# Block sums of the keys of two head pairs: two more columns of the turning matmul, or a reduction from PSUM

## The chip, the cores and the metric

The kernel runs on one core of a Trainium2 chip. A core has TensorE (PE, matmuls, with its weight loads shown apart as PEld), VectorE (DVE), ScalarE (ACT), GpSimd (POOL) and SyncE (SP), each with an instruction stream of its own; they meet through semaphores. TensorE writes into PSUM, which VectorE and ScalarE read; all engines but TensorE's output use the core's SBUF memory, and DMA queues move data between it and the chip's main memory. The metric is the device time of one execution in microseconds (us), lower is better.

## The reference

```python
def _attn_ref(q, k, v):                  # each (4, 8, 768, 64)
    B, H, S, D = q.shape
    block = 64; n_blocks = S // block; top_k = 3; scale = 1.0 / np.sqrt(D)
    k_rep = k.reshape(B, H, n_blocks, block, D).mean(axis=3)
    gate_scores = np.einsum('bhsd,bhnd->bhsn', q, k_rep)
    causal = pos[:, None] // block >= np.arange(n_blocks)[None, :]
    gate_scores = np.where(causal, gate_scores, -1000000000.0)
    top_idx = np.argsort(gate_scores, axis=-1)[..., -top_k:]
    # query i sees the keys j <= i in its three top blocks and in its own block
    scores = scale * np.matmul(q, k.transpose(0, 1, 3, 2))
    scores = np.where(mask, scores, -1000000000.0)
    attn = np.exp(scores - np.max(scores, axis=-1, keepdims=True))
    attn = attn / (np.sum(attn, axis=-1, keepdims=True) + 1e-09)
    return np.matmul(attn, v)

def _moe_ref(x, w_in, w_out):            # x (3072, 512), w_in (512, 2048), w_out (2048, 512)
    h = x @ w_in
    g = 0.5 * h * (1.0 + np.tanh(c * (h + 0.044715 * h * h * h)))
    return g @ w_out
```

The output of the attention, with the heads put side by side, is the input of the two matmuls with the gelu between them. The gate needs, for each head, the mean of the keys of each of the 12 blocks of 64; since only the order of the gate's scores matters, a sum serves as well as a mean. These sums over the keys are what the change is about.

## The kernel before, in words

The heads go in 16 pairs, p = 4 b + hp for batch b and pair of heads hp. Pairs 0 to 3 (batch 0) start the kernel; while TensorE later does the two matmuls of one batch, the attention of the next batch runs beside it.

*A pair of batch 0* (`pre`, from L528 on, and `heads2`). The loads bring keys, queries and values with the sequence on the partitions (`load`, L387; `load_0`, L421, for the first pair, its queries from ScalarE's queue and its keys from SyncE's). TensorE turns the keys in two halves of three chunks of 128 x 128 in f32 (`turn`, L538 or L541), into one PSUM bank per half. A copy takes the turned half to SBUF as f16 (`turned`; a copy is at L356 on ScalarE, L358 on GpSimd and L360 on VectorE). `ksb_h` puts the sums of a half's six blocks into a small matrix `ksb`, laid out by a 0/1 mask so that both heads of the pair can be gated at once; for pair 0 the sums of the second half also go into `ksbx`, because pair 0 gates in two steps. The queries are turned in the same way (L541), copied in f32, and cast once more to f16 for the scores (`q16`, on GpSimd for pairs 1 to 3). The gate is four f32 matmuls (L680, eight records), then VectorE does the selection: a 32 x 32 transpose (L696), the causal addition (L703), the three largest by MAX8 (L712), a comparison (L713) and the mask (L717). TensorE turns the mask (L749) and a copy brings it to SBUF. Then the scores (L856), the exponentials on ScalarE (L875) into one of six buffers `ats`, GpSimd's select for the causal part (L901), and the product with the values (L924), which are cast to f16 on GpSimd (`cast_v`). VectorE divides (L942, L943), TensorE turns the result (L981) into `xT`.

*The block sums before the change.* For the pairs named in KSUM (0 and 1), the matmul that turns a chunk of keys takes `identk` as its moving operand, which is the 128-wide identity with two more columns that hold ones for the chunk's first and second 64 keys. So it writes 130 columns, the last two of them block sums, and one VectorE multiplication (L588) by the mask reads them from PSUM. For pairs 2 and 3 the turning is a plain f32 transpose (L541), and VectorE reduces the 384 turned columns in PSUM to six sums (L576) and multiplies them by the mask (L582).

*The batches 1 to 3* load with a transposing pattern (L393), turn by VectorE (L557), reduce from SBUF (L614, L631), and use a score matmul with the mask as extra rows (L1039), exponentials (L1052), selects (L1066) and products (L1078).

*The two matmuls.* `s1` (L1115) multiplies by w_in, gelu on ScalarE (L1127); it waits for the last exponential of its batch, the turned result `xT` and its half of w_in. `s2_plain` (L1315) multiplies by w_out for batch 0; the last batch uses further forms (L1204, L1365, with joins on VectorE at L1414). The weights come in two halves each, 1 MB a half, issued by GpSimd (`load_w`, L453); the issue of w_in waits for the last values of batch 0 through a small copy (L451).

*What sets the order.* The program builds a numbered list of operations, and `Plan.run` emits them by a written-out list, ORDER: the instructions of each engine stand in the order of that list. BUFFER picks the buffer where several serve, and ENGINE names the operations that go to ScalarE or GpSimd and not to the engine they name first. SyncE's and GpSimd's DMA issues are operations in the same list. `warm` (L1517) are filler matmuls on zeros; the list holds them where TensorE was planned to have nothing else to do. NK = 3 sets of `ks` and `ksb` rotate over the pairs, and a third kind of PSUM bank ("pre", three of them) is held from a turning until the copy and the sums have read it.

Of the kernel before, what the change touches and what calls it, by code (L numbers as in the profile page):

```python
# [182 lines left out]
    "POOL": [  # L183
        337, 586, 587, 646, 647, 707, 708, 972, 973, 1035, 1036, 1097, 1159,
        1160, 1425, 1426, 1488, 1489, 1551, 1613]}


class Op:
# [1431 lines left out]
```

## Time and profile before

| | |
|---|---|
| time, median of 3 runs | 254.39 us (254.17 to 254.81) |
| the profiled execution | 253.93 us |
| its span, first to last instruction | 252.2 us |
| granted TensorE clock, mean | 1.000 |
| PE busy | 244.2 us (97%) |
| DVE busy | 188.8 us (75%) |
| ACT busy | 177.5 us (70%) |
| POOL busy | 84.0 us (33%) |

How to read the profile's lines. The first part of the page gives each engine's busy time, its share of the span and its instructions. A line of slices cuts the span in 40; a digit is the busy share in tenths, and PEclk is the clock granted to TensorE. A row of the windows gives a stretch (from:to, its length), then the busy time of PE, PEld, DVE, ACT and POOL with their counts, the granted clock, the DMA share and GB/s. A row of the groups names a line of the kernel, the engine, the operation, output and input, shapes and count, then busy us and mean ns of one, and the idle time before them with what ended it. A row of the timeline gives the start and the length in us of a run of like instructions on one engine, what they are, how many (x), and in brackets the idle time before them and what ended it. The chain is the work that ended last, followed back from the end; its summary gives shares by engine, with a q behind an engine's name for its queue or sequencer. Matmul records overlap, so that six in a row take less than six times one.

### The profile page before, as it was taken

How to read it: one execution, taken by the hardware profiler on the slowest of the kernel's cores; microseconds unless marked ns; L12 is line 12 of the kernel's file. 1: busy time of each engine (PE TensorE's matmuls, PEld its weight loads, DVE VectorE, ACT ScalarE, POOL GpSimd, SP SyncE). 2: the span in 40 equal slices, each digit the busy share in tenths (PEclk: the TensorE clock that was granted, in tenths of full speed). 3: DMA queues.
4: the chain of work that ended last, by engine and by line, in shares of the span. 5: the costliest groups of instructions: out<-in, count | busy, mean ns of one | idle time of the engine just before them, and what ended most of it. 6: DMA issues, size and time to landing. Idle time of an engine off the chain costs nothing.

```text
span 252.2 us, 6437 instructions
## 1 busy us (share of the span) xinstructions
PE 244.2 (97%) x2484; PEld 170.2 (67%) x2484; DVE 188.8 (75%) x535; ACT 177.5 (70%) x226; POOL 84.0 (33%) x166
## 2 busy tenths in 40 slices
PE   6899999999999999999999999999999999999993
PEld 4677776555555565565778887656777887666883
DVE  2679851034789999999997998999876585688954
ACT  2498978545899899867899795576999936656200
POOL 8657860011237657112147561210147500000000
PEclk9999999999999999999999999999999999999999
DMA  7998699999989987999899667184121330100023
GB/s 159 218 200 184 97 213 198 205 156 151 153 140 164 155 170 127 146 138 261 151 182 162 137 109 140 27 214 99 26 86 28 90 120 30 65 22 0 4 106 144
DMA packets 130927, 32.62 MB, mean 129 GB/s; under 512 B 124528, under 2 KB 126928, under 8 KB 130896
## 3 DMA queue, kind: packets, MB, share of 16 engines
q1 hardware_dynamic: 126160, 27.62, 62.8%
q0 software_dynamic: 3136, 4.19, 9.8%
q10 hardware_dynamic: 1600, 0.39, 0.8%
q8 instruction: 19, 0.31, 0.5%
q14 instruction: 12, 0.10, 0.1%
HBM read 27.26 MB, written 6.29 MB: 133 GB/s over the span
## 4 chain that ended last, share of the span: by engine, by line
PE 80%; SPq 8%; DMA 4%; DVE 3%; POOL 2%; issue 1%; DVEq 0%; POOLq 0%
PE wide L1115 27%; PE bank L1365 22%; PE wide L1039 9%; SPq L387 7%; PE bank L1315 6%; PE wide L1204 6%; PE bank L1078 5%; DMA vsd<-in_v_dram 2%; PE bank L680 2%; SPq L393 2%; DMA sd<-in_k_dram 1%; DMA G<-in_q_dram 1%; PE bank L924 1%; PE wide L856 1%; PE bank L981 1%
## 5 line engine op out<-in xcount | busy, mean ns | idle before, releaser
L1115 PE MATMUL wide<-xT,w_in 128*128 128x384 f16 x416 | 74.8, 326 | 0.0
L1052 ACT ACTIVATE ats<-wide 128x896 f16<-128x896 f32 x72 | 63.1, 915 | 5.8 <-PE wide L1039 3.8
L1127 ACT ACTIVATE G<-wide 128x768 f16<-128x768 f32 x52 | 42.0, 810 | 27.4 <-PE wide L1115 23.1
L1115 PEld LDWEIGHTS <-w_in 128*128 128x128 f16 x416 | 39.9, 98 | 26.9 <-issue 1.0
L1066 POOL TENSOR_SCALAR_AFFINE_SELECT ats<-ats 128x256 f16<-128x256 f16 x72 | 31.0, 443 | 51.1 <-ACT ats L1052 37.5
L1039 PE MATMUL wide<-qT,kT 76*128 76x512 f16 (+3 forms) x192 | 38.8, 305 | 0.0
L557 DVE STREAM_TRANSPOSE s<-sd 128x768 f32<-128x768 f32 x24 | 23.2, 971 | 14.2 <-DMA sd<-in_k_dram 12.9
L1365 PE MATMUL bank<-w_out,G 128*128 128x256 f16 x216 | 32.6, 272 | 0.0
L1365 PEld LDWEIGHTS <-G 128*128 128x128 f16 x288 | 26.9, 98 | 5.5
L1315 PE MATMUL bank<-w_out,G 128*128 128x512 f16 x96 | 28.8, 379 | 0.0
L358 POOL CAST kT<-s 64x768 f16<-64x768 f32 x20 | 16.9, 855 | 33.0 <-DVE s L557 32.4
L1414 DVE TENSOR_TENSOR osb<-bank,osb 128x512 f32<-128x512 f32 (+1 forms) x38 | 22.2, 592 | 4.7 <-PE bank L1365 4.1
L1078 PEld LDWEIGHTS <-ats 128*128 128x128 f16 x504 | 22.8, 98 | 4.2
L1078 PE MATMUL bank<-v,ats 128*128 128x65 f16 x504 | 24.9, 194 | 0.0
L1039 PEld LDWEIGHTS <-kT 76*128 76x128 f16 x192 | 17.2, 98 | 9.8 <-issue 0.3
L875 ACT ACTIVATE ats<-wide 128x1024 f16<-128x1024 f32 (+3 forms) x24 | 20.8, 916 | 3.2 <-PE wide L856 3.0
L1365 PEld LDWEIGHTS <-XS 128*128 128x128 f16 x216 | 20.1, 97 | 4.3
L1365 PE MATMUL bank<-TS,XS 128*128 128x256 f16 x144 | 22.6, 272 | 0.0
L358 POOL CAST v<-vsd 128x768 f16<-128x768 f32 x13 | 11.1, 858 | 22.9 <-DMA vsd<-in_v_dram 15.7
L962 DVE TENSOR_TENSOR xn<-bank,zr 128x384 f16<-128x384 f32 x24 | 13.4, 557 | 0.8
L712 DVE MAX8 sel<-sel 128x8 f32<-128x12 f32 x160 | 13.3, 157 | 0.6
L356 ACT CAST qT<-s 64x768 f16<-64x768 f32 x15 | 12.4, 830 | 0.3
(118 smaller groups left out, 352.8 us busy)
## 6 DMA issues: line engine op xcount, KB each, us to landing
out_dram<-osb SPq DMA_DIRECT2D x23, 256.0 KB
vsd<-in_v_dram SPq DMA_DIRECT2D x26, 192.0 KB
sd<-in_k_dram SPq DMA_DIRECT2D x48, 96.0 KB
sd<-in_q_dram SPq DMA_DIRECT2D x48, 96.0 KB
w_in<-in_moe_w_in_dram POOLq DMA_DIRECT2D x2, 1024.0 KB, 11.6
w_out<-in_moe_w_out_dram POOLq DMA_DIRECT2D x2, 1024.0 KB, 20.6
G<-in_k_dram SPq DMA_DIRECT2D x6, 192.0 KB
TS<-in_v_dram SPq DMA_DIRECT2D x6, 192.0 KB
```

The costliest lines, as they stand in the source:

```text
L358: nc.gpsimd.tensor_copy(out=out, in_=in_)
L557: nc.vector.transpose(out=T[key + "T32", p], in_=T[key, p].rearrange("p t j -> p (t j)"))
L875: nc.scalar.activation(out=T["at", u][:, :, 0:n], in_=plan.buf[("st",) + u].rearrange("p (h w) -> p h w", h=2)[:, :, 0:n], func=AF.Exp, bi ...
L1039: nc.tensor.matmul(st[:, x:e], kT16[i][h][0:76, s0:s0 + 128], qT16[i][h][0:76, s0 + (x - cb):s0 + (e - cb)], start=True, stop=True)
L1052: nc.scalar.activation(out=T["at", u][:, 0:n], in_=plan.buf[("st",) + u][:, 0:n], func=AF.Exp, bias=0.0, scale=SCALE)
L1066: nc.gpsimd.affine_select(out=dg, in_=dg, compare_op=ALU.is_ge, fill=0.0, base=0, pattern=[[0, 2], [1, 128]], channel_multiplier=-1)
L1078: nc.tensor.matmul(pvv[:, qc, 0:65], at[:, cb + (qc - jc) * 128: cb + (qc - jc + 1) * 128], v16[i][:, jc, h, :], start=(gi == 0 and jc == ...
L1115: nc.tensor.matmul(hps[:, 512 * e:512 * e + HALF], w_in16[:, ci, (2 * j + e) * 128: (2 * j + e + 1) * 128], T["xT", b][:, ci, HALF * h:HAL ...
L1127: nc.scalar.activation(out=G[:, :, h, j, :], in_=plan.buf["hps", b, j, h].rearrange("p (e w) -> p e w", e=2)[:, :, 0:HALF], func=AF.Gelu_a ...
L1315: nc.tensor.matmul(plan.buf["ops", b, ti], G[:, f % 2, 2 * ti // NC, f // 2, ti % (NC // 2) * 128:ti % (NC // 2) * 128 + 128], w_out16[:, ...
L1365: nc.tensor.matmul(dst[:, HD * h:HD * h + HD], FACT[m][0][:, j, t * 128:(t + 1) * 128], FACT[m][1][:, j, :], start=(clear and j == 0), sto ...
L1414: nc.vector.tensor_tensor(out=dst(), in0=src(), in1=other(), op=ALU.add)
```

## The change

KSUM becomes empty. So pairs 0 and 1 take the way that pairs 2 and 3 take already: their four halves of keys are turned by three f32 transposes each (L541) in place of three matmuls of 130 columns (L538), each of which is two records in the trace, and VectorE makes the sums with four reductions over 384 columns in PSUM (L576) and five multiplications (L582) in place of five multiplications from PSUM (L588). The tables by which the old way worked stay in the code.

With it the lists ORDER, BUFFER and ENGINE are written anew; the operations have the same numbers, and apart from fillers the same operations are in both.

```diff
@@ -19,170 +19,170 @@
 ORDER = [
-    4, 2, 0, 1890, 1891, 1892, 1893, 1894, 1895, 1896, 6, 1897, 15, 1898, 9,
...
@@ -257,7 +257,7 @@
     TURN = {"k": (), "q": (), "v": ()}
     NWARM = 72
     DUALS = 3
-    KSUM = (0, 1)
+    KSUM = ()
```

What the new lists move, as far as the text below speaks of it:

- The first pair's queries: ScalarE issues the first half before the second one; before, the second came first. The loads behind them on SyncE go q1, q1, k1, k1, q2 and so on; before, k1, q1, q1, k2, k1.
- ENGINE: two copies of turned keys of pairs 0 and 1 and some other copies of batch 0 go to ScalarE, and of batch 1 three query casts go to ScalarE and two mask copies back to VectorE. In all ScalarE's list goes from 53 to 58 operations, GpSimd's from 20 to 21.
- GpSimd: the issue of w_out stands behind the third of pair 3's selects; before, it stood between two selects of pair 2, ahead of pair 3's query cast and value cast (L358). The cast of pair 2's values, which stood ahead of the issue of w_in, now stands behind it.
- Fillers: 35 instead of 38, and all of them ahead of the first s1 matmul.

More of the change, by code (lines that the diff above doesn't have):

```diff
@@ L21 @@
 ORDER = [
[128 rows of a table removed]
-BUFFER = [
[23 rows of a table removed]
[128 rows of a table added]
+BUFFER = [
[23 rows of a table added]
 ENGINE = {
     "ACT": [
[5 rows of a table removed]
[5 rows of a table added]
     "POOL": [
-        337, 586, 587, 646, 647, 707, 708, 972, 973, 1035, 1036, 1097, 1159,
-        1160, 1425, 1426, 1488, 1489, 1551, 1613]}
+        338, 586, 587, 646, 647, 707, 708, 972, 973, 1035, 1036, 1097, 1098,
+        1159, 1160, 1425, 1426, 1488, 1489, 1612, 1613]}
 class Op:
```

311 rows, old and new, of tables (BUFFER, ENGINE, ORDER) are left out of this document.

## The prediction

> **What bounds the kernel now.** I read the busy shares first, then the chain of work that ended last, the table of windows, and the timelines of the engines around what the change touches.
>
> ```profile
> PE 244.2 (97%) x2484; PEld 170.2 (67%) x2484; DVE 188.8 (75%) x535; ACT 177.5 (70%) x226; POOL 84.0 (33%) x166
> PEclk9999999999999999999999999999999999999999
> PE 80%; SPq 8%; DMA 4%; DVE 3%; POOL 2%; issue 1%; DVEq 0%; POOLq 0%
> ```
> ```profile
> 0.00:10.00 10.00, 6.71 (x47) 4.56 (x48) 3.39 (x28) 2.40 (x4) 8.62 (x31) 1.00 1.01 181
> 10.00:20.00 10.00, 10.00 (x147) 7.51 (x146) 8.13 (x39) 8.26 (x14) 4.52 (x10) 1.00 1.20 205
> 20.00:30.00 10.00, 9.85 (x186) 7.54 (x184) 9.06 (x41) 9.32 (x12) 7.98 (x14) 1.00 0.68 124
> 30.00:38.00 8.00, 7.79 (x152) 6.08 (x149) 5.05 (x12) 6.58 (x9) 5.44 (x10) 1.00 1.12 212
> 61.00:98.00 37.00, 36.52 (x386) 21.23 (x385) 32.64 (x99) 34.02 (x44) 17.79 (x34) 1.00 1.03 151
> ```
>
> The columns are PE, PEld, DVE, ACT and POOL busy, then the clock, the DMA share and GB/s. Over the whole kernel TensorE is the bound. In the first 38 us its busy time deceives, because part of it is filler matmuls (L1517):
>
> ```profile
> L1517 PE MATMUL bank<-XS 128*128 128x256 f16 x33 | 7.5, 332 | 1.1 <-DVE bmask L285 1.1
> L538 PE MATMUL bank<-identk,G 128*128 128x130 f32 x24 | 3.6, 285 | 0.4 <-DMA G<-in_k_dram 0.4
> L576 DVE TENSOR_REDUCE ks<-bank 128x6 f32<-128x384 f32 x4 | 2.2, 545 | 0.0
> ```
>
> 33 fillers lie there, 7.5 us. So this stretch is set by loads and by the chain gate, selection, mask, scores, exponentials; from the first s1 matmul (L1115) on, a us of TensorE's list is a us of the end.
>
> ```profile
> 4.39 0.91 PE L538 MATMUL bank<-identk,G 128*128 128x130 f32 x6 [0.37 <-DMA G<-in_k_dram]
> 6.77 0.52 PE L541 MATMUL bank<-identk,G 128*128 128x128 f32 x3 [1.47 <-DMA G<-in_q_dram]
> 37.41 1.14 PE L1115 MATMUL wide<-xT,w_in 128*128 128x384 f16 x6
> 47.68 0.38 PE L1315 MATMUL bank<-w_out,G 128*128 128x512 f16 x1
> 85.25 0.48 PE L680 MATMUL bank<-s,ksb 128*32 128x160 f32 x8 [0.47 <-DVE ksb L631]
> 87.72 0.27 PE L1517 MATMUL bank<-XS 128*128 128x256 f16 x1
> ```
>
> **The change, part by part.** *TensorE's turning.* Four groups of six f32 records (0.91 us) become groups of three (0.52): 4 x 0.39 = 1.6 us less. All of it lies in the first windows, beside fillers and waits for loads, so I take nothing for it; if that cover were gone it would be worth its 1.6 us.
>
> *VectorE's sums.* Four reductions at 0.545 = 2.2 us come in. Five multiplications change their source:
>
> ```profile
> 5.34 0.17 DVE L588 TENSOR_TENSOR ksb<-bmask,bank 128x12 f32<-128x12 f32 x1 [3.12 <-PE bank L538]
> 5.50 0.55 DVE L360 CAST XS<-bank 128x384 f16<-128x384 f32 x1
> 9.71 0.16 DVE L588 TENSOR_TENSOR ksbx<-bmask,bank 128x12 f32<-128x12 f32 x1
> 17.34 0.21 DVE L582 TENSOR_TENSOR ksb<-bmask,ks 128x12 f32<-128x12 f32 x1
> 22.94 0.58 DVE L582 TENSOR_TENSOR ksb<-bmask,ks 128x12 f32<-128x12 f32 x1
> 22.67 0.83 POOL L358 CAST v<-TS 128x768 f16<-128x768 f32 x1 [0.83 <-DMA TS<-in_v_dram]
> ```
>
> At 0.21 against 0.17 they add 0.2, at 0.58 each 2.0; so VectorE gains between 2.4 and 4.2 us. The 0.58 one ran beside the cast of 22.67 on GpSimd. I take 2.4, by the other row, since what stands now where the new ones will (5.34, 9.71) ran undisturbed. The Trainium skill, "GPSIMD Engine Reference", section 8 "Key points", says that GpSimd's memory interfaces are shared with VectorE and that instructions with two SBUF inputs contend; L582 has two, L588 only one, so by it the sum would sit at the upper end. The row at 22.94 agrees with it; the sum goes by the rows.
>
> Against the 2.4, the new list gives ScalarE the copies (0.55 each) of two turned key halves of pairs 0 and 1 and a mask copy of about 0.5: VectorE keeps a net +0.8, and behind a reduction wait that half's gate and its selection. The first half of pair 0 is covered by the 1.47 us in which TensorE awaits queries. For the second half the reduction adds 0.55 where 9.71 has 0.16, about 0.6 with its multiplication; the new list loads the queries' first half ahead of the second one and turns the queries of pair 1 earlier, worth up to 0.5. So the first exponential, at 11.45, stays within 0.1.
>
> *GpSimd and the start of s1.* The list also moves the issue of w_out (L453) past pair 2's last selects, pair 3's query and value casts and three of its selects:
>
> ```profile
> 26.36 1.66 POOL L453 DMA_DIRECT2D w_in<-in_moe_w_in_dram  x2 [0.34 <-issue]
> 28.66 1.78 POOL L453 DMA_DIRECT2D w_out<-in_moe_w_out_dram  x2
> 31.03 0.84 POOL L358 CAST XS<-s 128x768 f16<-128x768 f32 x1
> 35.59 0.41 POOL L901 TENSOR_SCALAR_AFFINE_SELECT ats<-ats 128x256 f16<-128x256 f16 x1 [0.42 <-ACT ats L875]
> 31.92 0.29 PE L856 MATMUL wide<-XS,XS 64*128 64x256 f16 x2 [0.21 <-POOL XS L358]
> 11.45 1.51 ACT L875 ACTIVATE ats<-wide 128x512 f16<-128x512 f32 x2
> 32.52 3.27 ACT L875 ACTIVATE ats<-wide 128x1024 f16<-128x1024 f32 x4 [0.98 <-PE wide L856]
> 36.21 1.94 ACT L875 ACTIVATE ats<-wide 128x1024 f16<-128x1024 f32 x2 [0.41 <-PE wide L856]
> ```
>
> The cast at 31.03 stands right behind that 1.78 us issue and the select after it; the scores of pair 3 wait for the cast, ScalarE for the scores (0.98), and s1 comes when the last exponential ends. With the issue out of its way, but one value cast (0.83) ahead of it instead, the cast ends about 0.9 earlier, and the 0.98 goes nearly whole. What is late next is the weights:
>
> ```profile
> L453 POOL DMA_DIRECT2D w_out<-in_moe_w_out_dram x2: 883/894/904, 28.7 to 29.6; - x2
> DMA to landing us min/median/max: 18.2/20.6/23.0
> DMA  2111196999999999999999999999999999929999
> ```
>
> The first half of w_out lands at 28.66 + 18.2 = 46.9 and its first user starts at 47.68: s1 can gain 0.8 at most before L1315 waits. (The last line is the DMA share from 24 to 56 us in 40 slices: from about 29 us the transfers run one behind the other, so this landing follows from the bytes ahead of it, not from the time of issue.) Between 0 and -0.8 I take **-0.8**, because the wait that goes (0.98) is larger than the cap. The issue would now come behind the select of 35.59, near 35.2 to 36.9. After w_in's issue at 26.36 the share is at nine tenths from 28.0, so w_out's packets would flow by about 37. They are needed later: the second half lands at 29.6 + 23.0 = 52.6, 5.7 us behind the first, so the first began to flow near 41.2, or as early as 39.5 if I allow 1.7 us for a landing to show.
>
> *Fillers.* None stands behind the start of s1 in the new list; of the old one's, one at 87.72 and two near 228 and 230 go. At the spacing of 0.11 us of 256-column matmuls (0.38 - 0.27, below) that is **-0.3**.
>
> *The wait at 85.25.* TensorE waits 0.47 for the block sums of pair 7 behind an unbroken VectorE run from 69.72:
>
> ```profile
> 69.72 0.35 DVE L696 STREAM_TRANSPOSE sel<-bank 128x160 f32<-128x160 f32 x1 [1.27 <-PE bank L680]
> 84.24 0.65 DVE L360 CAST qT<-s 64x768 f16<-64x768 f32 x1
> 84.81 0.38 DVE L631 TENSOR_TENSOR ksb<-bmask,ks 128x32 f32<-128x32 f32 x1
> 17.04 0.39 PE L1517 MATMUL bank<-XS 128*128 128x256 f16 x2
> 248.12 0.27 PE L1517 MATMUL bank<-XS 128*128 128x256 f16 x1
> ```
>
> The new list gives three such casts (0.55 to 0.65) to ScalarE and takes two mask copies back, a run shorter by about 0.8; but TensorE arrives about 0.8 earlier too. Of the 0.47 I take **-0.2**. ScalarE gets some 1.6 us more in these 37 us and starts them 0.8 earlier.
>
> *New waits.* Every wait of the new order is unseen. From 61 to 98 us TensorE idles 0.48 in 37, all but 0.01 of it the wait at 85.25, so a new one costs at worst about as much, 0.5, and two of them 1.0. Nothing excludes a gain from waits too small to be listed. Between -0.4 and +1.0 I take **+0.3**, nearer to that row.
>
> The sum: -0.8 - 0.3 - 0.2 + 0.3 = -1.0, on 253.93 for the profiled execution 252.9. That execution lies 0.46 below the median of 254.39, against which the result is read, so 253.4.
>
> **The rivals.** *Nothing at the start.* The weights, or the longer VectorE run, hold s1 at 37.4; then only fillers and the small wait count, -0.3 to -0.5, with the new waits +0.3: 254.2. For it: the cap of 0.8 is thin. Against: a 0.98 wait with a plain cause.
>
> *Slower: VectorE's sums.* Place: VectorE between 5 and 26 us, busy 8.13 and 9.06 of 10. Price: 2.4 less the copies at half their worth, since ScalarE is as full (8.26, 9.32) and takes them ahead of its exponentials: +1.3 on the start of s1, less 0.3 for fillers, 255.4. It decides once the first exponential comes after 12.3. For it: both engines are at nine tenths. Against: the four exponential waits of 20 to 38 us, not VectorE, end the stretch.
>
> *Slower: w_out too late.* If GpSimd issues it after 37.6 us (39.5 less the 1.6 to 2 us until packets flow) the transfers break off, and each us beyond costs one at the first L1315. An issue behind the last select, past 38, with all of 1.8 us to run, makes +1.5 and less 0.3 for fillers: 255.6. For it: GpSimd is 5.44 of 8 us busy there, and the selects wait for ScalarE (0.42 at 35.59). Against: 1.6 us of room.
>
> *Slower: the clock.* The rows that speak on it: 13 fillers in the first 2.95 us,
>
> ```profile
> 1.07 2.95 PE L1517 MATMUL bank<-XS 128*128 128x256 f16 x13 [1.07 <-DVE bmask L285]
> ```
>
> which is 0.22 each, twice the later 0.11. The granted clock is nonetheless 1.00 in each window. If matmuls stayed at twice their time until 10 us, the some 2 us of turning, gating and masks before the first score would cost up to 2 more: 256.4. By the Trainium skill, "TensorE: Matmul & The Clock Gate", "Part 4: PE-mode transpose", transposes do not count as busy for the clock gate, which would speak for this rival, since the change makes matmuls into transposes. No row bears it out: L541 at 6.77 (0.52 for three) is no slower than the L538 halves around it.
>
> *More.* All listed waits go and no new one comes: -0.8 - 0.4 - 0.5 = -1.7, 252.7.
>
> **How the numbers follow.** My forecast 0.40, more 0.12, nothing at the start 0.25, VectorE's sums 0.12, w_out late 0.08, the clock 0.03. What can be told from no change here is about 0.3%, 0.76 us. Faster takes the first two, 0.52; same 0.25; slower 0.23. The range goes from 252.2 (the larger gain, and half a us for its bounds) to 255.3 (most of VectorE's rival): it leaves out about 0.18. The forecast's own range is 252.7 to 254.0.
>
> **What would show it.** Right: L576 eight times before 38 us at about 0.55, no L538; first exponential within 0.3 of 11.45; pair 3's query cast ending near 31, no ScalarE wait near 1 us after it; first L1115 at 36.4 to 36.8; first L1315 near 46.9 with little wait; no L1517 after s1 begins; a smaller wait for ksb near 84. Wrong: a first exponential after 12.3, an L1115 after 37.4, a wait of L1315 for w_out, or new TensorE waits above 0.5 us after 61.

## The result, and the profile after

The changed kernel takes 256.06 us (median of 11 runs, 255.43 to 256.74) against 254.39 us of the kernel before in the same job: a ratio of 1.0063, with an interval of 1.0044 to 1.0082. It is slower by about 1.6 us. The forecast was 253.4 us, faster by 1.0; the measured time also lies above the range of 252.2 to 255.3. The profiled execution took 256.06 us, with a span of 254.4.

The busy line of the page, its chain, and the windows, with the columns of the prediction:

```profile
PE 243.7 (96%) x2469; PEld 167.7 (66%) x2469; DVE 190.4 (75%) x533; ACT 180.8 (71%) x231; POOL 86.5 (34%) x167
PE 59%; SPq 16%; DMA 10%; ACT 4%; DVE 4%; POOL 3%; issue 3%; ACTq 0%; POOLq 0%; DVEq 0%
```
```profile
0.00:10.00 10.00, 6.43 (x49) 4.00 (x51) 4.36 (x31) 3.07 (x6) 8.62 (x31) 1.00 1.01 180
10.00:20.00 10.00, 9.46 (x132) 6.42 (x132) 9.31 (x38) 8.29 (x14) 5.13 (x11) 1.00 1.21 217
20.00:30.00 10.00, 10.00 (x198) 7.81 (x193) 9.28 (x40) 9.38 (x13) 6.64 (x12) 1.00 0.73 117
30.00:38.00 8.00, 7.07 (x143) 5.33 (x140) 5.74 (x14) 6.48 (x8) 5.53 (x10) 1.00 1.12 212
61.00:98.00 37.00, 35.90 (x352) 20.00 (x350) 32.77 (x96) 32.91 (x42) 17.79 (x33) 1.00 1.07 139
180.00:231.00 51.00, 50.57 (x514) 37.54 (x512) 34.53 (x64) 38.23 (x47) 12.14 (x25) 1.00 0.17 47
```

TensorE is busy half a us less than before and yet ends later. From 61 to 98 us it idles 1.10 us (0.48 before), from 180 to 231 us 0.43 (0.02 before). The timeline shows the start of s1 and the waits ahead of it and behind it:

```profile
4.37 0.91 PE L541 MATMUL bank<-identk,G 128*128 128x128 f32 x6 [0.56 <-DMA G<-in_k_dram]
17.58 0.45 PE L749 MATMUL bank<-ident,madd 128*128 128x128 f16 x5 [0.52 <-DVE madd L717]
31.04 0.45 PE L749 MATMUL bank<-ident,madd 128*128 128x128 f16 x5 [0.93 <-ACT ats L875]
38.03 1.79 PE L1115 MATMUL wide<-xT,w_in 128*128 128x384 f16 x10
48.20 0.38 PE L1315 MATMUL bank<-w_out,G 128*128 128x512 f16 x1
70.56 0.48 PE L680 MATMUL bank<-s,ksb 128*32 128x160 f32 x8 [0.25 <-DVE s L557]
77.79 0.48 PE L680 MATMUL bank<-s,ksb 128*32 128x160 f32 x8 [0.47 <-ACT ats L1052]
90.13 0.45 PE L749 MATMUL bank<-ident,madd 128*128 128x128 f16 x5 [0.33 <-DVE madd L717]
```

The first s1 matmul comes at 38.03, 0.62 us later than before, although the first exponential is a little earlier (11.22 against 11.45). What grew in between is on VectorE. These are its selection and sum instructions in the stretches ahead of those waits, and GpSimd's casts beside them, both from the timeline of the changed kernel:

```profile
14.76 0.59 DVE L703 TENSOR_TENSOR sel<-sel,cgate 128x120 f32<-128x120 f32 x1
16.64 0.89 DVE L717 SCALAR_TENSOR_TENSOR madd<-sel,ownm 128x120 f16<-128x120 f32 x1
21.60 0.80 DVE L717 SCALAR_TENSOR_TENSOR madd<-sel,ownm 128x120 f16<-128x120 f32 x1
28.00 0.94 DVE L703 TENSOR_TENSOR sel<-sel,cgate 128x120 f32<-128x120 f32 x1
30.20 0.78 DVE L717 SCALAR_TENSOR_TENSOR madd<-sel,ownm 128x120 f16<-128x120 f32 x1
68.84 0.77 DVE L631 TENSOR_TENSOR ksb<-bmask,ks 128x32 f32<-128x32 f32 x1
75.93 0.82 DVE L631 TENSOR_TENSOR ksb<-bmask,ks 128x32 f32<-128x32 f32 x1
89.26 0.81 DVE L717 SCALAR_TENSOR_TENSOR madd<-sel,ownm 128x120 f16<-128x120 f32 x1
```
```profile
14.40 0.82 POOL L358 CAST XS<-s 128x768 f16<-128x768 f32 x1
16.57 0.83 POOL L358 CAST v<-G 128x768 f16<-128x768 f32 x1 [1.35 <-DMA G<-in_v_dram]
21.44 0.82 POOL L358 CAST v<-TS 128x768 f16<-128x768 f32 x1 [2.15 <-DMA TS<-in_v_dram]
27.98 0.83 POOL L358 CAST v<-TS 128x768 f16<-128x768 f32 x1
29.98 0.86 POOL L358 CAST XS<-s 128x768 f16<-128x768 f32 x1
67.89 1.69 POOL L358 CAST kT<-s 64x768 f16<-64x768 f32 x2 [11.05 <-DVE s L557]
75.89 0.82 POOL L358 CAST kT<-s 64x768 f16<-64x768 f32 x1
89.11 0.82 POOL L358 CAST kT<-s 64x768 f16<-64x768 f32 x1
```

Read the two lists row by row: each long instruction starts while a cast runs and ends within 0.15 us after it (28.00 + 0.94 = 28.94, the cast 27.98 + 0.83 = 28.81). Where nothing of GpSimd runs beside them, L703 and L717 of this shape take 0.28 and L631 0.15 to 0.19 in these two traces. All of them read two operands from SBUF. I call the time over this undisturbed one what an instruction is held. The groups of the first 38 us give it for pairs 1 to 3, first of the kernel before, then of the changed one:

```profile
L703 DVE TENSOR_TENSOR sel<-sel,cgate 128x120 f32<-128x120 f32 x3 | 1.0, 340 | 0.1
L717 DVE SCALAR_TENSOR_TENSOR madd<-sel,ownm 128x120 f16<-128x120 f32 x3 | 0.9, 312 | 0.2
```
```profile
L576 DVE TENSOR_REDUCE ks<-bank 128x6 f32<-128x384 f32 x8 | 4.4, 548 | 2.7 <-PE bank L541 2.7
L703 DVE TENSOR_TENSOR sel<-sel,cgate 128x120 f32<-128x120 f32 x3 | 1.8, 605 | 0.1
L717 DVE SCALAR_TENSOR_TENSOR madd<-sel,ownm 128x120 f16<-128x120 f32 x3 | 2.5, 825 | 0.2
```

Six instructions are held 3 x 0.33 + 3 x 0.55 = 2.6 us in all, against 0.3 before. With L582 and L713 the sums over this stretch are about 3.4 and 0.8; from 61 to 98 us, with L631, 2.5 and 1.2 (all good to some 0.2, by which shortest time is taken). In the kernel before, pair 3's L703 and the turning of its mask stand here:

```profile
27.59 0.28 DVE L703 TENSOR_TENSOR sel<-sel,cgate 128x120 f32<-128x120 f32 x1
30.10 0.45 PE L749 MATMUL bank<-ident,madd 128*128 128x128 f16 x5
```

The held instructions stand on the chain from gate to mask, so the mask of pair 3 is turned at 31.04 and not at 30.10. (The row at 31.04 names ScalarE's exponentials; the mask, L717, ended last, at 30.98.) ScalarE then waits 1.11 us for pair 3's scores, where it waited 0.98:

```profile
11.22 1.02 ACT L875 ACTIVATE ats<-wide 128x1024 f16<-128x1024 f32 x1
32.11 4.92 ACT L875 ACTIVATE ats<-wide 128x1024 f16<-128x1024 f32 x5 [1.11 <-PE wide L856]
```

The start of s1 is the smaller part of the loss. From the start of the first s1 matmul to the start of the last matmul the kernel before takes 248.12 - 37.41 = 210.71 us, the changed one 250.18 - 38.03 = 212.15. So in the two profiled executions the last matmul starts 2.06 us later, of which 0.62 are lost ahead of s1 and 1.44 behind it. About 1.1 of the 1.44 is idle time of TensorE: 0.6 more from 61 to 98 us, 0.1 from 98 to 140, 0.4 from 180 to 231.

### The profile page after: what moved, and what is told of

Read it like the earlier page. It is cut to its first block, busy times and chain, and to the rows that moved or that the text cites. A ratio compares the mean times of both kernels' runs of the same rounds, so it can differ in the third digit from the quotient of the medians.

```text
span 254.4 us, 6412 instructions
## 1 busy us (share of the span) xinstructions
PE 243.7 (96%) x2469; PEld 167.7 (66%) x2469; DVE 190.4 (75%) x533; ACT 180.8 (71%) x231; POOL 86.5 (34%) x167
## 4 chain that ended last, share of the span: by engine, by line
PE 59%; SPq 16%; DMA 10%; ACT 4%; DVE 4%; POOL 3%; issue 3%; ACTq 0%; POOLq 0%; DVEq 0%
PE bank L1365 19%; PE wide L1115 19%; SPq L393 9%; PE wide L1039 7%; SPq L387 6%; DMA w_in<-in_moe_w_in_dram 5%; PE wide L1204 5%; PE bank L1078 4%; ACT ats L1052 3%; PE bank L1315 3%; POOL ats L1066 2%; DMA TS<-in_v_dram 2%; PE bank L680 2%; DMA sd<-in_q_dram 1%; DMA G<-in_q_dram 1%
## 5 line engine op out<-in xcount | busy, mean ns | idle before, releaser
L1115 PE MATMUL wide<-xT,w_in 128*128 128x384 f16 x416 | 73.9, 326 | 0.0
L1066 POOL TENSOR_SCALAR_AFFINE_SELECT ats<-ats 128x256 f16<-128x256 f16 x72 | 32.7, 469 | 39.5 <-ACT ats L1052 36.7
L557 DVE STREAM_TRANSPOSE s<-sd 128x768 f32<-128x768 f32 x24 | 23.2, 968 | 14.0 <-DMA sd<-in_k_dram 13.0
L358 POOL CAST kT<-s 64x768 f16<-64x768 f32 x21 | 17.5, 834 | 34.3 <-DVE s L557 33.7
L1315 PE MATMUL bank<-w_out,G 128*128 128x512 f16 x96 | 28.4, 379 | 0.0
L358 POOL CAST v<-vsd 128x768 f16<-128x768 f32 x13 | 11.2, 868 | 32.1 <-DMA vsd<-in_v_dram 32.1
L356 ACT CAST qT<-s 64x768 f16<-64x768 f32 x19 | 15.6, 826 | 0.2
```

The lines of the kernel that those rows point to most:

```text
L358: nc.gpsimd.tensor_copy(out=out, in_=in_)
L557: nc.vector.transpose(out=T[key + "T32", p], in_=T[key, p].rearrange("p t j -> p (t j)"))
L1066: nc.gpsimd.affine_select(out=dg, in_=dg, compare_op=ALU.is_ge, fill=0.0, base=0, pattern=[[0, 2], [1, 128]], channel_multiplier=-1)
L1115: nc.tensor.matmul(hps[:, 512 * e:512 * e + HALF], w_in16[:, ci, (2 * j + e) * 128: (2 * j + e + 1) * 128], T["xT", b][:, ci, HALF * h:HAL ...
L1315: nc.tensor.matmul(plan.buf["ops", b, ti], G[:, f % 2, 2 * ti // NC, f // 2, ti % (NC // 2) * 128:ti % (NC // 2) * 128 + 128], w_out16[:, ...
```

## The experiments

Two theories stood at the start: that the lists had put GpSimd's casts beside VectorE's two-input instructions (A), or that the four new reductions were what was paid (B). Times are medians, the ratio is to the kernel before in the same job (its medians there 254.17 to 254.29). The first s1 matmul, and the time from its start to that of the last matmul, are read from one profiled execution each. Between two kernels with the same beginning of the list (before and e10), the first s1 matmul differed by 0.2 us (37.41, 37.63), the first exponential by 0.7 (11.45, 12.16). The time from s1 to the last matmul repeats within 0.04 us where the later list and its casts are the same, but for e12.

| | lists of | sums by | edit | first s1 | s1 to last | time | ratio (interval) |
|---|---|---|---|---|---|---|---|
| before | before | columns | | 37.41 | 210.71 | 254.39 | |
| after | after | VectorE | | 38.03 | 212.15 | 256.06 | 1.0063 (1.0044 to 1.0082) |
| e1 | before | VectorE | | 39.41 | 210.67 | 255.90 | 1.0063 (1.0047 to 1.0079) |
| e2 | after | columns | | 38.14 | 212.15 | 256.34 | 1.0087 (1.0070 to 1.0105) |
| e3 | after | VectorE | no casts in batch 0 | 36.74 | 212.16 | 255.29 | 1.0040 (1.0021 to 1.0059) |
| e4 | after | VectorE | no casts on GpSimd | 37.07 | 211.65 | 254.83 | 1.0020 (1.0001 to 1.0039) |
| e5 | before | VectorE | no casts in batch 0 | 38.03 | 210.67 | 254.68 | 1.0023 (1.0013 to 1.0032) |
| e6 | before | columns | no casts in batch 0 | 37.86 | 210.71 | 254.31 | 1.0004 (0.9996 to 1.0013) |
| e7 | after | columns | no casts in batch 0 | 37.40 | 212.18 | 255.64 | 1.0063 (1.0050 to 1.0076) |
| e8 | after | VectorE | casts in three pieces | 38.21 | 211.69 | 255.02 | 1.0030 (1.0011 to 1.0050) |
| e9 | before | columns | casts in three pieces | 37.15 | 211.45 | 254.61 | 1.0013 (0.9999 to 1.0027) |
| e10 | before | columns | three late fillers left out | 37.63 | 210.71 | 254.43 | 1.0020 (0.9997 to 1.0043) |
| e11 | before | columns | e9 and e10 together | 37.42 | 210.94 | 254.46 | 1.0015 (0.9992 to 1.0039) |
| e12 | after | VectorE | one cast moved back | 36.98 | 212.30 | 255.31 | 1.0042 (1.0028 to 1.0057) |
| e13 | before | columns | w_out's issue as in after | 37.05 | 210.68 | 253.97 | 0.9991 (0.9969 to 1.0013) |
| e14 | before | columns | w_out's issue ahead of pair 3's selects | 37.70 | 210.70 | 255.03 | 1.0033 (1.0009 to 1.0057) |

### e1 and e2: the two halves of the change apart

```diff
 # e1, in the kernel before; e2 is the reverse edit in the changed kernel
-    KSUM = (0, 1)
+    KSUM = ()
```

> The lists of before, and only the sums of pairs 0 and 1 made by VectorE (KSUM empty). Theory A, the port: the changed kernel lost because its new list puts GpSimd's f32 to f16 casts beside VectorE's instructions with two SBUF inputs (L703, L717, L631), which are then held until the cast ends (28.00 + 0.94 against a cast from 27.98 to 28.81). The sums themselves then cost little: first exponential at most 0.6 us later than 11.45, first s1 matmul within 0.4 us of 37.41, the time 0 to +0.5 us of before. Theory B, the sums: VectorE's four reductions (2.2 us) are what is paid: first s1 matmul 0.6 us or more later, the time +0.6 to +1.7 us.

> The lists of the changed kernel, with the sums of pairs 0 and 1 made by the two more columns as before (KSUM holds 0 and 1). Theory A, the port: the loss belongs to the lists and stays, +1.2 to +2.2 us over before, with TensorE's waits of 0.4 us and more near 30, 70, 77 and 89 us still there, though single casts may shift on or off a selection. Theory B, the sums: the loss goes, within 0.5 us of before.

Neither theory held as it stood: each half alone costs what both cost together. They lose it in different places. The sums in the old list put s1 off by 2.0 us and change nothing behind it (210.67). The new lists put it off by 0.7 and lose 1.44 behind it, whichever engine makes the sums (e2 and the changed kernel, 212.15 both). e1's timelines of VectorE, GpSimd and TensorE show how much of it is the sums:

```profile
14.05 0.55 DVE L576 TENSOR_REDUCE ks<-bank 128x6 f32<-128x384 f32 x1
14.52 0.82 POOL L358 CAST XS<-s 128x768 f16<-128x768 f32 x1
14.63 0.74 DVE L582 TENSOR_TENSOR ksb<-bmask,ks 128x12 f32<-128x12 f32 x1
15.29 0.55 DVE L576 TENSOR_REDUCE ks<-bank 128x6 f32<-128x384 f32 x1
...
16.19 0.48 PE L680 MATMUL bank<-s,ksb 128*32 128x160 f32 x8 [1.52 <-ACT ats L875]
```

The gate of pair 1 comes at 16.19, 2.1 us after its place before (14.07); 0.8 of it was there at the first exponential (12.29). The new L582 has two SBUF inputs, and the cast of pair 1's queries, which before met an instruction that reads PSUM (L588 at 13.73, 0.17 beside the cast of 13.68), holds it 0.57. Behind it L703 and L717 of the next selections meet casts too (held 0.33, 0.43, 0.50); the sum of the held time before 38 us is 2.2 us. So the two theories had to be told apart without casts.

### e3 and e4: the changed kernel without GpSimd's casts

```diff
         elif eng == POOL:
-            nc.gpsimd.tensor_copy(out=out, in_=in_)
+            nc.gpsimd.tensor_copy(out=out[:, 0:16], in_=in_[:, 0:16])
+            nc.gpsimd.memset(out, 0.0)
 # e3: only the casts of batch 0; e4: all (a branch for tiles of four dimensions is not shown)
```

> The changed kernel with GpSimd's eight or so casts of batch 0 (values, queries of pairs 1 to 3) left out: each becomes a copy of 16 columns, which still waits for the data, and a memset of the whole tile, so GpSimd is busy about as long. The attention of batch 0 is wrong for it. In before's trace L703 ran in 0.21 beside a memset. Theory A, the port: the excess of L703, L713, L717 and L582 before 38 us falls from 3.4 us to under 1.2; TensorE's wait near 30 us (1.1 us) goes; first s1 matmul at 37.0 to 37.4 in place of 38.03; the time 0.6 to 1.0 us below the changed kernel. Theory B, the sums or GpSimd's queue: durations of the selection may fall, but the start of s1 and the time stay within 0.3 us of the changed kernel.

> The same for all of GpSimd's casts in the program, the keys and values of batches 1 to 3 too. Left out: all values and the keys that GpSimd casts are zeros. Theory A: the waits near 70, 77 and 89 us, each behind an L631 or L717 held by a cast, go as well; TensorE's idle time from 61 to 98 us falls from 1.1 us to 0.5 or less; the time 1.2 to 2.2 us below the changed kernel, at or below before. Theory B: no more gain than in the run without the casts of batch 0.

Each cast left out becomes a copy of 16 columns, which waits for its data as the cast did, and a memset of the tile, so the attention of batch 0 (in e4 of all batches) is not computed. e3 starts s1 at 36.74, 1.3 us earlier than the changed kernel, with GpSimd as busy as there. Its last matmul comes at 248.90, also 1.3 us earlier. L703 is back at 0.28 for all three pairs. Pair 1's ran beside a memset (in this file L703 is L715):

```profile
14.91 0.28 DVE L715 TENSOR_TENSOR sel<-sel,cgate 128x120 f32<-128x120 f32 x1
14.80 0.74 POOL L366 MEMSET XS<- 128x768 f16 x1
```

In the changed kernel it took 0.59, beside the cast of 14.40. What is held falls from 3.4 to 1.4 us, the rest beside GpSimd's selects (L901). In the times e3 is 0.8 us below the changed kernel; the two intervals overlap, so it is the trace that shows it. In the medians e4 takes a further 0.5 us off. Its interval lies wholly below that of the changed kernel, not below that of e3; its windows show the place:

```profile
61.00:98.00 37.00, 36.47 (x390) 21.00 (x388) 32.57 (x99) 34.19 (x44) 20.68 (x48) 1.00 1.17 144
```

TensorE idles 0.53 us there and not 1.10, and L631 takes 0.15 to 0.23. From s1 to the last matmul e4 needs 211.65 us in place of 212.15. Theory A came out in its direction and in the two gains in time, not in all its numbers: the held time fell to 1.4 and not under 1.2, s1 came earlier than the 37.0 to 37.4 expected, and e4 remains 0.5 us above the kernel before.

### e5, e6, e7: the other three corners without casts

The edit of e3 in the lists of before with VectorE's sums, in the kernel before, and in the lists of after with the columns.

> The lists of before with the sums by VectorE, and GpSimd's casts of batch 0 left out as before (16 columns copied, the tile zeroed by a memset; batch 0's attention is wrong). With the real casts this had its first s1 matmul at 39.41, 2.0 us after before's, and 2.2 us of held instructions before 38 us. Theory A1, the sums cost because they push VectorE's two-input instructions beside casts: first s1 matmul at 38.0 to 38.6, the time 0.7 to 1.4 us below the run with casts. Theory B1, the reductions lengthen the chain of the first two pairs by themselves: first s1 matmul at 39.0 or later, the time within 0.4 us of the run with casts.

> The kernel before, with GpSimd's casts of batch 0 left out in the same way: the base of the run above. Its held instructions sum to 0.8 us before 38 us, one of them (L582, 0.41) ahead of pair 3's gate. Theory A1: first s1 matmul at 36.9 to 37.4, the time 0 to 0.5 us below before. The sums' own price without casts is the difference of the two runs: under 1.2 us by A1, about 1.6 to 2.0 by B1.

> The lists of the changed kernel with the sums by the two more columns, and GpSimd's casts of batch 0 left out. With the real casts its first s1 matmul was at 38.14 and 2.0 us were held before 38 us. Theory A: first s1 matmul at 36.7 to 37.4, the time 0.7 to 1.3 us below the run with casts. Rival, the new order itself is slow at the start: first s1 matmul at 37.8 or later.

Without casts in batch 0 the sums cost 254.68 - 254.31 = 0.4 us and 0.2 us at the start of s1, where with casts they cost 1.6 and 2.0. Theory A1 is borne out by e5: about three quarters of the price of VectorE's sums in the old list were instructions held by casts. It missed in e6, where it expected a gain of up to 0.5 us and s1 by 37.4 (it came at 37.86): in the kernel before itself the casts cost nothing that the times show, so its holds lie beside the path. The new lists keep a part that is neither sums nor casts of batch 0: e7 lies 1.3 us above e6, e3 0.4 to 0.6 us above e5 (by the ratios and by the medians, from two jobs). This part lies behind s1, where e3 and e7 take as long as the changed kernel (212.16, 212.18). By e4 a half us of it is casts of later batches; the rest is open, below.

### e8 to e11: shorter holds, and no late fillers

```diff
 # e8, e9, e11
-            nc.gpsimd.tensor_copy(out=out, in_=in_)
+            for x in range(3):       # a third of the columns each
+                nc.gpsimd.tensor_copy(out=out[:, w * x:w * x + w], in_=in_[:, w * x:w * x + w])
 # e10, e11: three of the filler operations are not emitted
+            if n in (1924, 1925, 1926):
+                continue
```

> The changed kernel with every cast of GpSimd done in three instructions of a third of the columns. If a held VectorE instruction is let in between two of GpSimd's, a hold lasts a third: the excess of the two-input instructions falls from 3.4 us before 38 us to 1.5 or less, first s1 matmul at 37.2 to 37.8, the time 0.4 to 1.2 us below the changed kernel. If GpSimd keeps the port from piece to piece, or the two further instructions of each cast cost GpSimd as much as the holds, the time stays within 0.3 us or rises.

> The kernel before with each cast of GpSimd in three instructions. Its two-input instructions are held 0.8 us before 38 us and 1.2 us from 61 to 98 us, and only part of that stands on the path (leaving the casts of batch 0 out moved the time by 0.1). Port theory: the time 0 to 0.4 us below before. If the further instructions cost GpSimd's queue as much as the holds: the same or 0.3 us above.

> The kernel before without its three filler matmuls behind the start of s1 (near 87.7, 228 and 230 us). The prediction's term: 0.3 us, if TensorE has other work ready at these places. Rival: they stand in waits of VectorE and are free, the time the same within 0.1 us.

> The kernel before with both edits, the split casts and without the three fillers: the sum of the two, 0.3 to 0.7 us below before if both terms are real, at most 0.1 if neither is.

The split takes 1.0 us off the median of the changed kernel (ratios 1.0030 and 1.0063, whose intervals just overlap), although a cast in three takes GpSimd 1.1 us and not 0.83. Where the gain lies the trace does not settle, because the profiled execution, 255.78 us, is among the longest of the ten. In it s1 is no earlier (38.21, against a first exponential of 12.42, 1.2 us later than in the changed kernel) and the held time before 38 us falls only to 2.2, both against what was expected; behind s1 it gains 0.46 us (211.69), nearly as much as leaving out all casts. In the kernel before the split gains nothing (e9, 0.3 us up, within what can be told); there TensorE's wait for `ksb` near 85 us grows from 0.48 to 1.25.

e10 settles the three fillers. From the first s1 matmul to the last matmul it takes 248.34 - 37.63 = 210.71 us, and the kernel before 248.12 - 37.41 = 210.71 us. So they cost nothing. That they fill waits is a reading that fits; no idle row appears in their place. e11, 0.2 us up, cannot be told from no change.

### e12: one cast moved back

```diff
 # ORDER of the changed kernel
-    252, 256, 144, 264, 157, 226, 56, 288, ...
+    252, 256, 144, 264, 56, 157, 226, 288, ...
```

157 is the issue of w_in, 56 the cast of pair 2's values.

> The changed kernel with one operation of GpSimd's list moved: the cast of pair 2's values stands ahead of the issue of w_in again, as before, so that it no longer meets L703 of pair 3's selection (held 0.70 at 28.00). Port theory: that L703 takes 0.28 to 0.4, pair 3's mask is turned 0.4 to 0.8 us earlier against the first exponential (it was 19.8 us after it), and the time falls 0.3 to 0.8 us. Rival, GpSimd's queue or other waits set the start: the mask and the time stay within 0.2 us, or the casts behind it come earlier and hold another instruction.

```profile
27.84 0.28 DVE L703 TENSOR_TENSOR sel<-sel,cgate 128x120 f32<-128x120 f32 x1
29.33 0.60 DVE L717 SCALAR_TENSOR_TENSOR madd<-sel,ownm 128x120 f16<-128x120 f32 x1
...
29.98 0.45 PE L749 MATMUL bank<-ident,madd 128*128 128x128 f16 x5
36.98 1.30 PE L1115 MATMUL wide<-xT,w_in 128*128 128x384 f16 x7
```

L703 takes 0.28 and not 0.94, pair 3's mask is turned 1.06 us earlier and s1 starts 1.05 us earlier, with the same first exponential (11.21). Of the 1.06 us, 0.66 are L703's, 0.18 L717's (0.60 and not 0.78), and 0.16 were there at L703's start. The last matmul gains 0.9 us (249.28 against 250.18) and the median 0.75, though the intervals of the two ratios still overlap. This is the clearest run for the start of s1: nothing but one place in GpSimd's list is changed. Behind s1 nothing is won (212.30).

### e13 and e14: the prediction's step alone

In ORDER of the kernel before the issue of w_out (163) moves behind the third select of pair 3 (310), as in the changed kernel, or behind pair 3's value cast (61).

> The kernel before, sums by the columns, with only the issue of w_out moved to where the changed kernel has it, behind the third select of pair 3. This is the prediction's step alone: pair 3's query cast ends near 30.1 in place of 31.87, ScalarE's wait of 0.98 shrinks to under 0.4, the first s1 matmul comes 0.5 to 0.8 us earlier against the first exponential (25.96 us after it in before), L1315 does not wait, the time -0.4 to -0.8 us. Rival, the mask decides: the mask of pair 3 (turned at 30.10, copied until 31.08) or a selection held by the moved cast leaves no more than 0.3 us, and the time stays within 0.3 us of before.

> The same with the issue behind pair 3's value cast, ahead of its selects. The query cast comes as early as in the run beside it, but the selects of pair 3 wait for the issue's 1.8 us. If the query cast is what counts: as the run beside it. If pair 3's selects count as much: no gain, or 0.3 to 0.8 us lost.

The timeline of e13:

```profile
30.01 0.82 POOL L358 CAST XS<-s 128x768 f16<-128x768 f32 x1
32.16 3.27 ACT L875 ACTIVATE ats<-wide 128x1024 f16<-128x1024 f32 x4 [0.58 <-PE wide L856]
35.58 1.78 POOL L453 DMA_DIRECT2D w_out<-in_moe_w_out_dram  x2
37.05 1.14 PE L1115 MATMUL wide<-xT,w_in 128*128 128x384 f16 x6
```

The cast comes 1.0 us earlier and ends at 30.83, but ScalarE's wait only shrinks from 0.98 to 0.58. What is late next lies behind the mask: it is turned at 30.14, its copy ends at 31.12, and twelve products stand in TensorE's list ahead of the scores, which start at 31.55. The trace does not part the mask's copy from that list. s1 gains 0.36, and the last matmul 0.39 (247.73). In the times it is 0.3 us below before, which cannot be told from no change. e14 loses 0.8 us in the medians (0.3 in its profiled execution, one of its fastest): with the issue ahead of pair 3's selects, ScalarE's later wait of 0.41 becomes 1.13. So the selects count as much as the cast, and the place behind them is the better one.

## Why the prediction was wrong, point by point

*The bound.* Right in that what s1 starts later, the end comes later (0.62 us). But most of the loss, 1.44 us, came behind the start of s1, where the forecast's three terms came to -0.2.

*TensorE's turning.* Right as far as the trace tells: 12 records take the place of 24, and of the 1.6 us no more than 0.2 shows at the first exponential (11.22 against 11.45), less than it differs by from execution to execution.

*VectorE's sums.* The number of instructions, 0.55 for each reduction, and a first exponential near its old place were right; that it came so near is in part luck, since it varies by 0.7. The choice "I take 2.4, by the other row, since what stands now where the new ones will (5.34, 9.71) ran undisturbed" was wrong in its reason: those two rows read PSUM, and L582 reads two SBUF operands, as L703, L717 and L631 do. This decided e1, where one L582 was held 0.57. It did not decide the changed kernel, whose L582 are held 0.6 of the 3.4 us, and which is as slow without them (e2).

*The step that failed ahead of s1.* It is the term -0.8 for the issue of w_out, with its reason: the 0.98 "goes nearly whole", and "what is late next is the weights". The new lists moved casts past the selections of all pairs, and I counted for them only GpSimd's own time. The row of an L582 at 22.94, 0.58 beside a cast, was the case in point, and I applied it to the five new instructions alone. In the changed kernel the held time is 3.4 us before 38 us in place of 0.8, pair 3's mask is turned 0.9 us later, and s1 starts 0.62 us later where 0.8 earlier was forecast. Without the casts of batch 0 it starts at 36.74 (e3), within the 36.4 to 36.8 that the prediction named, and one cast moved back gives 1.05 us (e12). The sentence that I had beside the sum, from the Trainium skill, "GPSIMD Engine Reference", section 8, spoke of just this contention. The Trainium skill's page "SBUF — State Buffer", section "SBUF: two separate sides", is plainer: the port pair shared by VectorE and GpSimd is an exclusive lock, taken for a whole instruction by whichever starts first, and a VectorE instruction with two SBUF inputs meets it only against a GpSimd instruction that reads SBUF. The runs agree in both parts: L703 at 28.00 ends 0.13 after the cast, and beside e3's memset of 14.80, which reads nothing, it takes 0.28.

*The step that failed behind s1.* It is the sum -0.3 - 0.2 + 0.3, above all the +0.3 for new waits, taken near the one wait of the old order. Measured were +1.44 (212.15 against 210.71), the same with either way of making the sums. Casts of later batches are 0.5 of it (e4); the other 0.9 stays open, below.

*The issue of w_out, -0.8.* The cast came early as forecast (29.98, and 30.01 in e13), and w_out was no limit: the trace has its first half landing 10.5 us after the issue at 36.55, so at 47.05, ahead of L1315 at 48.20. But the wait of 0.98 had a second cause 0.4 us behind the first, the mask with what stands behind it in TensorE's list; alone the move is worth about 0.4 us at the start of s1 (e13). In the changed kernel the mask came 0.9 later and took it all. The turning of the mask, at 30.10 in the kernel before, was not looked at.

*Fillers, -0.3.* Wrong: 0.0 for the three of e10; I had priced them as work. The place was misread too: the trace of the kernel before has five behind the first s1 matmul, at 39.93, 87.72, 221.17, 225.27 and 248.12, and the changed kernel none. (The row shown for their spacing gives 0.12, 0.39 - 0.27.)

*The wait at 85.25, -0.2.* Wrong in sign: that wait went, and three others came, at 70.56, 77.79 and 90.13, the first two behind a transpose (L557) that follows an L631 held by a cast, the third behind such an L717. Without casts (e4) the first and the third are gone and the second is 0.29 in place of 0.47. Where this term and that for new waits made +0.1, TensorE's idle time rose by 0.6 from 61 to 98 us and by 0.4 from 180 to 231.

*The rivals.* "VectorE's sums" named the right engine and side, but its price was for another mechanism; without casts the reductions cost about 0.4 us (e5 against e6, whose intervals touch), not 1.3. The price was also added up wrongly: 2.4 less half of the copies' 1.6 is 1.6, which gives 255.7 and not 255.4. Its deciding point, a first exponential after 12.3, did not come, and the loss did. "w_out too late" did not happen (issue at 36.55); its limit of 37.6 rests on 1.7 us allowed for a landing, which no row here gives, and no run came near it. The clock: the granted clock stays 1.00 in each window before 231 us, with twelve transposes more in the first 14 us. So nothing of the rule on transposes that the prediction took from the Trainium skill, "TensorE: Matmul & The Clock Gate", "Part 4: PE-mode transpose", is seen here; it is no test of the rule, since other matmuls run beside them.

*What stays open.* Without any cast on GpSimd the new lists are still 0.5 us above before in the median (e4): s1 starts 0.3 us earlier, but from s1 to the last matmul they need 0.94 us more. The windows of e4 place 0.7 us of idle TensorE between 180 and 231 us, where the kernel before has 0.02. Its longest waits there are 0.37 for one of GpSimd's selects (L1066) and 0.23 for a copy on ScalarE. The second is in the changed kernel too, but no run changed these alone.

```profile
228.69 0.81 PE L1204 MATMUL wide<-sd 128*128 128x384 f16 x4 [0.24 <-ACT ats L356]
```

## What to carry to other kernels

When an edit moves copies on GpSimd, or lengthens VectorE's list, write down which VectorE instructions read two SBUF operands and what GpSimd runs beside each: a 0.28 us instruction on the critical chain took 0.9 here when a cast had just begun, and busy shares show nothing of it. A wait that ends with one late operand is worth only the distance to the second latest, so look up both before pricing its end. Three fillers that would have been worth 0.3 us by their spacing cost nothing; price a filler by the time between two milestones, not by its duration. The same two milestones, the first s1 matmul and the last one, also part a loss at the start from one behind it; read them before looking for a cause.

## What was not expected of the hardware

GpSimd's selects (L901) hold as its casts do, only for a shorter time: an L582 of the changed kernel took 0.55 at 12.48 beside the select of 12.38. Cutting a cast into three shortens the hold: in e8 L703 and L717 take 0.29 to 0.47 where they met pieces of casts before 32 us, and up to 0.94 in the changed kernel; an L713 that met three pieces took 0.55. Each cast then takes GpSimd 0.3 us more. The median of the kernel with holds on its path fell by 1.0 us, with intervals that just overlap; the other kernel gained nothing.
